# The transposed state of a chunked recurrence: by a transposition stage, or by a second product with swapped operands, in a chain of four stages

## The chip, the cores and the metric

The kernel runs on one core of a Trainium2 chip. The metric is the device time of one execution in microseconds (us). It is measured over several executions, and the median is given. One further execution is recorded by the hardware profiler; all lines of the profile are from that one.

## What is computed

Two parts follow each other. The first is a recurrence over 768 tokens for 4 x 8 = 32 heads, each with a state of 40 x 40; the second is a dense layer pair of 320 x 2048 and 2048 x 320 over all 3072 tokens, with a piecewise quadratic activation between.

```python
def _attn_ref(r, k, v, w, a, b):              # each 4 x 8 x 768 x 40, f32
    state = np.zeros((B, H, D, D))
    for t in range(S):
        y[:, :, t] = np.einsum('bhd,bhde->bhe', rt, state)
        Sa = np.einsum('bhde,bhe->bhd', state, at)
        state_decay = state * wt[:, :, None, :] - np.einsum('bhd,bhe->bhde', Sa, bt)
        state = state_decay + np.einsum('bhd,bhe->bhde', vt, kt)
...
def _moe_ref(x, w_in, w_out):                 # 3072 x 320, 320 x 2048, 2048 x 320
    h = x @ w_in
    g = np.where(h >= 1, h, np.where(h <= -1, 0.0, (h + 1) ** 2 / 4))
    return g @ w_out
```

## The kernel before

**Chunks and halves.** The 768 tokens are cut into 24 chunks of 32. The heads are handled in two halves of 16. For one half of one chunk, `chain(c, hb)` (line 441) makes the output of the chunk and the state for the next chunk. It is a Python generator: each `next` on it issues one stage, up to the next `yield`. All matrix work in it is on small f32 tiles, one or two matmuls for each of 16 heads; the profile counts every f32 matmul as two instructions, so a group of 16 shows as x32.

The five stages of the chain before are:

1. L456: 16 products into one PSUM tile, and L460, a ScalarE copy into `x0`.
2. L466: 16 products with the inverted 32 x 32 matrices `tinv`. VectorE (L473) and ScalarE (L477) then take turns to put the results into the operand tile `cg`, four instructions each, from one PSUM tile.
3. L484: 16 products with all 128 rows, which give both the chunk's output (columns 0 to 31) and the new state (columns 32 to 71). VectorE scales the state by the decay into the next chunk's operand tile `cn` (L491, four instructions) and the output into `yt` (L496, two).
4. L513: the new state, 40 x 40 for each head, is transposed by a product with an identity; ScalarE copies it to `ss` (L517). `round_y` (L502) splits the output into two parts for the dense layers, on ScalarE and GpSimd.
5. L523: 16 products of the transposed state with the next chunk's rows `pn`; ScalarE copies the result to `cn` (L525, two instructions). With that, stage 1 of the next chunk can start.

**What feeds the chain.** For each half chunk, `load_cg` and `load_ti` issue DMAs on SyncE's queue that bring rows from a scratch buffer in DRAM, `turn` (parts 0, 1, 2) makes three groups of 32 x 32 transposes on VectorE (L410, L413, L415), and `scores` makes 32 small products (L425) and masks them on VectorE (L434). There are three operand tiles `cg`, so that a half chunk is loaded while two others are in use.

**The dense layers** are the generator `moe()` (line 558). A group is 64 tokens of each batch row, 256 columns; there are 12 groups. For each of 16 blocks of 128 hidden units, TensorE makes eight matmuls of 256 columns into `ph` (L594; two such PSUM tiles take turns), ScalarE applies Relu and Square (L600, L601), and six matmuls of 320 columns (L568, L572) of the block two before are made. Then VectorE finishes the activation (L607), which is also the last reader of `ph`, so the block after next cannot begin its L594 before that L607. ScalarE (L581) and GpSimd (L582) split the activation into two parts. `feed(cols)` (line 809) draws matmuls from this generator until their columns, counted by its `yield`s, reach what is owed. In one chunk's time 30720 columns are owed, which is half a group, so the dense layers keep pace with the chain. They start in chunk 2 with a delay, and end after it.

**Background.** `background(n)` draws from three more generators for later chunks: `rows` (running products of the decays on VectorE, L234 and L243, products on GpSimd, loads and a store), `ab` (32 x 32 transposes L278, products L289) and `inv` (triangular inversion on GpSimd, L314 and L320). Each has windows of time in tenths of a chunk (`WINDOWS`), and `SHARE` says how a chunk's share is spread over its ten steps. `adopt` (L328) turns an inverse into `tinv` every fourth chunk. `pull(wgen, 2)` draws from the conversion of the dense weights, which is done in the first chunks.

**What sets the order.** The order of each engine's instructions is that in which the code issues them (`manual_schedule`); each engine works its queue in order. The loop at line 833 has ten steps in a chunk. A step is one stage of one half, and then three times 1024 columns of the dense layers and a slice of the background. Odd steps belong to half 0, even ones to half 1; in steps 2 and 4 that is still half 1 of the chunk before.

All short-lived PSUM tiles come from one pool of four (`psum()`, line 62).

## Time and profile before

| What | us |
|---|---|
| median of 3 runs | 941.84 (938.14 to 942.95) |
| the profiled execution | 939.9 |
| its span, first to last instruction | 937.4 |
| TensorE busy in the span | 740.5 |
| VectorE busy in the span | 606.9 |
| ScalarE busy, GpSimd busy | 456.3, 428.4 |

The span is 2.5 us less than the time of the profiled execution, since it leaves out what lies ahead of the first and behind the last instruction. PE stands for TensorE, PEld for its weight loads, DVE for VectorE, ACT for ScalarE, POOL for GpSimd, SP for SyncE. A row of the timeline gives the start, how long it took, the engine, line and operation, `out<-in`, the sizes, how many equal instructions are merged, and in brackets how long the engine had stood idle and what ended that. Matmuls overlap, so the durations of rows that follow each other run a little into one another. The "PEclk" column is the granted TensorE clock as a share of full speed.

### The profile page before, as it was taken

The page shows a single profiled execution, that of the slowest core. Times are in us where ns is not written, and L with a number is a line of the kernel's source. Part 1 is how long each engine was busy: PE and PEld are TensorE (multiplying, and loading weights), DVE is VectorE, ACT ScalarE, POOL GpSimd, SP SyncE. Part 2 cuts the span into 40 slices and gives each one's busy share as a digit, 9 for nine tenths or more (in the row PEclk, how much of TensorE's full clock was granted, in tenths as well). Part 3 has the DMA queues.
Part 4 walks back from the last instruction along what each step waited for, and adds up shares of the span by engine and source line. Part 5 has one row for each costly group of instructions (what it writes and reads, how often), then busy time and mean ns, then how long its engine had stood idle before and what let it go on. Part 6 is the DMA issues. An engine that isn't in the chain of part 4 may idle for free.

```text
span 937.4 us, 35480 instructions
## 1 busy us (share of the span) xinstructions
PE 740.5 (79%) x14976; PEld 654.3 (70%) x14976; DVE 606.9 (65%) x1574; ACT 456.3 (49%) x1182; POOL 428.4 (46%) x673
## 2 busy tenths in 40 slices
PE   4343542348988986988796988899999999999995
PEld 3232532337877875877785977788888888888895
DVE  5787877577766784777755776666766566665321
ACT  5453444123444433545353544446556555656663
POOL 4300223677323696334695332796226952223332
PEclk9565555577977989899899889989999999999998
DMA  9299993665896556786467685575733554451000
GB/s 305 55 199 254 218 221 103 143 135 122 185 190 142 136 132 120 150 183 141 77 146 140 125 183 115 102 164 103 144 89 71 120 102 95 84 110 37 19 30 14
DMA packets 223167, 122.01 MB, mean 130 GB/s; under 512 B 142825, under 2 KB 214697, under 8 KB 223009
## 3 DMA queue, kind: packets, MB, share of 16 engines
q1 hardware_dynamic: 219808, 108.61, 54.5%
q0 software_dynamic: 3200, 11.14, 3.9%
q8 instruction: 117, 1.92, 0.9%
q14 instruction: 42, 0.34, 0.1%
HBM read 90.54 MB, written 27.53 MB: 126 GB/s over the span
## 4 chain that ended last, share of the span: by engine, by line
PE 37%; DVE 23%; DMA 12%; POOL 8%; ACT 7%; issue 6%; SPq 6%; DVEq 0%; ACTq 0%; POOLq 0%
PE ph L594 12%; PE po L568 7%; PE p L484 4%; PE po L572 4%; DVE arena L234 3%; PE p L513 3%; DVE cg L473 3%; SPq L265 3%; DVE qt L607 2%; DVE rec L243 2%; ACT cg L477 2%; POOL lw L314 2%; POOL lw L320 2%; DMA ti<-scr 2%; DMA ld_a<-in_a_dram 2%
## 5 line engine op out<-in xcount | busy, mean ns | idle before, releaser
L594 PE MATMUL ph<-X,w 120*128 120x256 f32 x1536 | 260.2, 305 | 62.3 <-DVE qt L607 61.1
L582 POOL TENSOR_TENSOR gl<-qt,gh 128x256 fp32r<-128x256 f32 x192 | 141.2, 736 | 299.4 <-ACT gh L581 284.5
L594 PEld LDWEIGHTS ph<-X,w 120*128 120x128 f32 x1536 | 215.4, 200 | 83.0 <-DVE qt L607 67.9
L568 PE MATMUL po<-wide,gh 128*128 128x320 f32 x768 | 161.9, 327 | 0.3 <-ACT gh L581 0.3
L607 DVE SCALAR_TENSOR_TENSOR qt<-qt,ph 128x256 f32<-128x256 f32 x192 | 79.9, 416 | 124.0 <-ACT qt L601 111.9
L581 ACT CAST gh<-qt 128x256 fp32r<-128x256 f32 x192 | 78.0, 406 | 160.3 <-DVE qt L607 159.7
L477 ACT ACTIVATE cg<-p 32x160 f32<-32x160 f32 x192 | 56.5, 294 | 149.5 <-DVE cg L473 149.5
L568 PEld LDWEIGHTS po<-wide,gh 128*128 128x128 f32 x768 | 123.2, 200 | 3.6 <-ACT gh L581 0.5
L484 PE MATMUL p<-cg 128*64 128x72 f32 (+1 forms) x1536 | 74.4, 259 | 44.2 <-ACT cg L477 43.5
L473 DVE SCALAR_TENSOR_TENSOR cg<-p,mask 32x128 f32<-32x128 f32 x192 | 55.3, 288 | 78.5 <-ACT cg L477 52.0
L572 PE MATMUL po<-wide,gl 128*128 128x320 f32 x384 | 97.9, 333 | 7.9 <-POOL gl L582 7.7
L484 PEld LDWEIGHTS p<-cg 128*64 128x64 f32 x1536 | 65.6, 163 | 55.0 <-ACT cg L477 46.0
L600 ACT ACTIVATE qt<-ph,half_c 128x256 f32<-128x256 f32 x192 | 90.9, 473 | 20.2 <-POOL gl L582 14.3
L434 DVE TENSOR_TENSOR cg<-p,mask 32x256 f32<-32x256 f32 x192 | 80.6, 420 | 19.2 <-PE p L425 16.4
L320 POOL TENSOR_TENSOR lw<-lw 128x31 f32<-128x31 f32 (+15 forms) x155 | 83.7, 540 | 8.3
L601 ACT ACTIVATE qt<-qt 128x256 f32<-128x256 f32 x192 | 80.2, 418 | 6.1
L314 POOL TENSOR_TENSOR lw<-lw 128x31 f32<-128x31 f32 (+15 forms) x155 | 78.8, 509 | 8.5
L491 DVE SCALAR_TENSOR_TENSOR cg<-p,pr 40x160 f32<-40x160 f32 x184 | 59.1, 321 | 28.4 <-PE p L484 26.4
L572 PEld LDWEIGHTS po<-wide,gl 128*128 128x128 f32 x384 | 65.2, 195 | 13.4 <-POOL gl L582 10.6
L513 PE MATMUL p<-ident,cg 40*64 40x40 f32 x1472 | 57.5, 238 | 1.5 <-issue 1.5
L513 PEld LDWEIGHTS p<-ident,cg 40*64 40x64 f32 x1472 | 51.8, 146 | 3.6 <-issue 1.6
L466 PE MATMUL p<-x,tinv 32*32 32x72 f32 x1536 | 38.5, 242 | 10.8 <-DVE tinv L328 8.7
(106 smaller groups left out, 997.4 us busy)
## 6 DMA issues: line engine op xcount, KB each, us to landing
ti<-scr SPq DMA_DIRECT2D x96, 200.0 KB
ti<-scr SPq DMA_DIRECT2D x96, 168.0 KB
scr<-arena POOLq DMA_DIRECT2D x16, 640.0 KB, 5.6
cg<-scr SPq DMA_DIRECT2D x96, 80.0 KB
X<-Y SPq DMA_DIRECT2D x36, 160.0 KB
scr<-wide SPq DMA_DIRECT2D x8, 640.0 KB
tiab<-scr SPq DMA_DIRECT2D x32, 160.0 KB
scr<-in_r_dram SPq DMA_DIRECT2D x24, 160.0 KB
```

What stands on the lines that cost most here:

```text
L314: eng.tensor_mul(t3, W3[:, 0:n, j : j + 1].broadcast_to([128, n, m]), L3[:, j + 1 :, j].unsqueeze(1).broadcast_to([128, n, m]),)
L320: eng.tensor_sub(W3[:, 0:n, j + 1 :], W3[:, 0:n, j + 1 :], t3)
L434: nc.vector.tensor_tensor(out=cg[q, f::2, C_X : C_X + 64][:, 4 * i : 4 * i + 4].rearrange("p h (j x) -> p h j x", x=32), in0=ps[quarter(f, ...
L473: nc.vector.scalar_tensor_tensor(out=cg[q, f + 2 * i :: 4, C_R : C_R + 32], in0=psv[quarter(f, i), :, 0:32], scalar=-1.0, in1=mask[quarter ...
L484: nc.tensor.matmul(psv[h // 8][64 * f : 64 * f + 64, h // 2 % 4, 0:n3], lhsT=cgw[:, h * CW + C_G : h * CW + C_G + 64], rhs=cg[:, h, C_R : ...
L513: nc.tensor.matmul(pst[64 * f : 64 * f + 64, p, :], lhsT=cn[er[f], h, C_S : C_S + 64], rhs=ident[er[f]], start=True, stop=True)
L568: nc.tensor.matmul(pos[i], lhsT=gh[:, ts_], rhs=w2[f // 8][:, j, f % 8, :], start=f == 0 and j == 0, stop=False)
L572: nc.tensor.matmul(pos[i], lhsT=gl[:, ts_], rhs=w2[f // 8][:, 0, f % 8, :], start=False, stop=f == NF - 1)
L582: nc.gpsimd.tensor_sub(gl, gt, gh.bitcast(F32))
L594: nc.tensor.matmul(ph, lhsT=w1[:, wi, fs], rhs=Xs[g][:, xi, :], start=i == 0, stop=i == 7)
L600: nc.scalar.activation(gt, ph, AF.Relu, bias=half_c, scale=0.5)
L607: nc.vector.scalar_tensor_tensor(out=gt, in0=gt, scalar=1.0, in1=ph, op0=ALU.min, op1=ALU.max)
```

## The change

The transposition stage goes. The state is made by a product of two operands, and the same product with its operands swapped gives its transpose, so stage 3 now makes both: 16 new products (L486 of the changed kernel) into one PSUM tile, copied by ScalarE to `ss` in two instructions of 40 partitions (L491), ahead of the products that give output and state (now L497). The decay, which the transposed copy lacks, is applied where the last stage's result is taken out of PSUM: VectorE does that now (L528, two instructions of 40 x 256), in place of ScalarE's copy (L525 before). `round_y` moves to that stage. Stage 2 writes two PSUM tiles, so that VectorE and ScalarE read different ones at a time.

The loop over chunks now has four parts instead of ten steps. In each, two stages are issued one behind the other, one of each half, which stand two stages apart: third and first, fourth and second. Behind them stand the loads, `turn`, `scores` and `adopt`, and then `fill()`: six times 1280 columns of the dense layers, each with a slice of the background. `SHARE` has four entries. The columns in a chunk stay 30720, and `pull(wgen, 2)` is drawn 12 times in a chunk, not 10.

```diff
-SHARE = (3.1, 1.45, 0.93, 2.03, 0.6) * 2
+SHARE = (1.4, 0.6) * 2
+SLOTS = len(SHARE)
...
-        psv = psum()[:, 0:288].rearrange("p (h x) -> p h x", x=72)
+        psv = [psum()[:, 0:288].rearrange("p (h x) -> p h x", x=72) for _ in range(2)]
...
-                psv[quarter(f, p % 2), p // 2, :], lhsT=tinv[q : q + 32, c % 4, 4 * hb + p // 2, :],
+                psv[p % 2][quarter(f, p % 2), p // 2, :], lhsT=tinv[q : q + 32, c % 4, 4 * hb + p // 2, :],
...
         yield
+        if not last:
+            pst = psum()[:, 0:320].rearrange("p (h x) -> p h x", x=40)
+            for h in range(16):
+                nc.tensor.matmul(
+                    pst[er[h % 2], h // 2, :], lhsT=cg[:, h, C_S : C_S + D], rhs=cg[:, h, C_G : C_G + D], start=True, stop=True
+                )
+            ss = work.tile([128, 8, 40], F32, tag="ss", name="ss", bufs=1)
+            for rows in er:
+                nc.scalar.copy(ss[rows], pst[rows])
         psv = psum_2()
...
-        pst = psum()[:, 0:320].rearrange("p (h x) -> p h x", x=40)
-        for h in range(16):
-            f, p = h % 2, h // 2
-            nc.tensor.matmul(
-                pst[64 * f : 64 * f + 64, p, :], lhsT=cn[er[f], h, C_S : C_S + 64], rhs=ident[er[f]], start=True, stop=True
-            )
-        ss = work.tile([128, 8, 40], F32, tag="ss", name="ss", bufs=1)
-        nc.scalar.copy(ss, pst)
-        round_y()
-        yield
...
         for f in range(2):
-            nc.scalar.copy(cn[er[f], f::2, C_R : C_R + 32], psv[er[f]])
+            nc.vector.scalar_tensor_tensor(
+                out=cn[er[f], f::2, C_R : C_R + 32], in0=psv[er[f]], scalar=-1.0,
+                in1=pr[er[f], :, 1, 39:40].broadcast_to([D, 8, 32]), op0=ALU.mult, op1=ALU.mult,
+            )
+        round_y()
         yield
...
+    def fill():
+
+        for k in range(6):
+            feed(1280)
+            if k % 2 == 0:
+                pull(wgen, 2)
+                if first:
+                    first.pop(0)()
+            background(now[0] + 10 / SLOTS * (k + 1) / 6)
+        now[0] += 10 / SLOTS
```

The loop over chunks after the change, whole:

```python
    for c in range(NC + 1):
        nxt = c + 1 < NC
        if c < NC:
            gens[c, 0] = chain(c, 0)
            gens[c, 1] = chain(c, 1)
        stage(c - 1, 1)
        stage(c, 0)
        if 0 < c < NC:
            if c % 4 == 0:
                adopt(c // 4)
            for j in (1, 2):
                turn(c, 1, j)
            if nxt:
                load_ti(c + 1, 1)
        fill()
        stage(c - 1, 1)
        stage(c, 0)
        if 0 < c < NC:
            scores(c, 1)
        for g, (t0, nt) in enumerate(groups):
            if t0 + nt == 32 * c:
                reclaim(5 + g % 2)
                Xs[g] = relayout(g)
                if idle[0]:
                    owed[0], idle[0] = -TRAIL * 3072, False
        if c == NC:
            break
        if nxt:
            load_cg(c + 1, 0)
            turn(c + 1, 0, 0)
        fill()
        stage(c, 0)
        stage(c, 1)
        if nxt:
            for j in (1, 2):
                turn(c + 1, 0, j)
            if c + 2 < NC:
                load_ti(c + 2, 0)
        fill()
        stage(c, 0)
        stage(c, 1)
        if nxt:
            scores(c + 1, 0)
            load_cg(c + 1, 1)
            turn(c + 1, 1, 0)
        fill()
```

The rows below show the order in which instructions stand in an engine's queue, late in the program (about chunk 20), where no background is left on VectorE. First VectorE before, for about half a chunk: `cg_83` to `cg_85` are the three operand tiles, `ph_63` and `ph_64` the two PSUM tiles of the dense layers, `p_` tiles those of the pool of four.

```order
L434 TENSOR_TENSOR cg_85<-p_12120,mask 32x4x64 x4
L410 STREAM_TRANSPOSE cg_83<-ti_80 64x8x32 x2
L473 SCALAR_TENSOR_TENSOR cg_84<-p_12202,mask 32x4x32 x4
L607 SCALAR_TENSOR_TENSOR qt<-qt,ph_63 128x256
L413 STREAM_TRANSPOSE ev<-ti_80 128x512
L607 SCALAR_TENSOR_TENSOR qt<-qt,ph_64 128x256
L491 SCALAR_TENSOR_TENSOR cg_83<-p_12288,pr_87 40x4x40 x2
L491 SCALAR_TENSOR_TENSOR cg_83<-p_12289,pr_87 40x4x40 x2
L496 TENSOR_TENSOR yt<-p_12288,pr_87 128x128
L496 TENSOR_TENSOR yt<-p_12289,pr_87 128x128
L607 SCALAR_TENSOR_TENSOR qt<-qt,ph_63 128x256
L415 STREAM_TRANSPOSE pr_86<-ti_80 128x16x32
```

VectorE at the same place after the change (L614 is L607 of before, L477 is L473, L438 is L434, L414 to L419 are L410 to L415, L504 is L491, L528 is new):

```order
L417 STREAM_TRANSPOSE ev<-ti_80 128x512
L419 STREAM_TRANSPOSE pr_88<-ti_80 128x16x32
L614 SCALAR_TENSOR_TENSOR qt<-qt,ph_63 128x256
L614 SCALAR_TENSOR_TENSOR qt<-qt,ph_64 128x256
L528 SCALAR_TENSOR_TENSOR cg_85<-p_12990,pr_86 40x8x32 x2
L477 SCALAR_TENSOR_TENSOR cg_84<-p_13011,mask 32x4x32 x2
L477 SCALAR_TENSOR_TENSOR cg_84<-p_13012,mask 32x4x32 x2
L438 TENSOR_TENSOR cg_85<-p_13037,mask 32x4x64 x4
L414 STREAM_TRANSPOSE cg_83<-ti_81 64x8x32 x2
L614 SCALAR_TENSOR_TENSOR qt<-qt,ph_63 128x256
L614 SCALAR_TENSOR_TENSOR qt<-qt,ph_64 128x256
L504 SCALAR_TENSOR_TENSOR cg_83<-p_13144,pr_87 40x4x40 x2
```

Before, three or fewer groups of chain work stood between two activations of the dense layers; now the activations stand in pairs, and all of a part's chain work stands between two pairs. The first of a pair, on `ph_63`, belongs to the block that TensorE made last in the part before.

TensorE before, from one activation tile to the next (L425 is `scores`, L513 the transposition, L466 stage 2):

```order
L594 MATMUL ph_63<-X_1761,w_89 128x256 x4
L425 MATMUL p_12120<-cg_85,ev 32x32 x16
L425 MATMUL p_12120<-pr_88,ev 32x32 x16
L513 MATMUL p_12157<-ident,cg_85 64x40 x16
L594 MATMUL ph_63<-X_1761,w_89 128x256 x4
L568 MATMUL po_65<-wide_884,gh 128x320 x2
L568 MATMUL po_66<-wide_884,gh 128x320 x2
L572 MATMUL po_65<-wide_884,gl 128x320
L572 MATMUL po_66<-wide_884,gl 128x320
L466 MATMUL p_12202<-x_12083,tinv 32x72 x16
L594 MATMUL ph_64<-X_1761,w_89 128x256 x8
```

TensorE after, in a part with a third and a first stage (L486 are the swapped products, L497 output and state, L460 stage 1; L601, L575 and L579 are L594, L568 and L572):

```order
L486 MATMUL p_12112<-cg_83 40x40 x16
L497 MATMUL p_12132<-cg_83 64x72 x8
L497 MATMUL p_12133<-cg_83 64x72 x8
L460 MATMUL p_12157<-cg_84 32x72 x16
L601 MATMUL ph_64<-X_1823,w_89 128x256 x8
L575 MATMUL po_65<-wide_884,gh 128x320 x2
L575 MATMUL po_66<-wide_884,gh 128x320 x2
L579 MATMUL po_65<-wide_884,gl 128x320
L579 MATMUL po_66<-wide_884,gl 128x320
L601 MATMUL ph_63<-X_1823,w_89 128x256 x8
```

Chain and dense layers were interleaved in pieces of 3072 columns; now a part has its two stages first, and then two whole blocks of the dense layers (7680 columns), the one on `ph_64` and then the one on `ph_63`.

More of the change, by code (lines that the diff above doesn't have):

```diff
@@ L356, in window, with gone @@
         return WINDOWS[key][s - 1]
-    gone = lambda x: sum(SHARE) * (int(x) // 10) + sum(SHARE[: int(x) % 10]) + SHARE[int(x) % 10] * (x % 1)
+    def gone(x):
+        x = x * SLOTS / 10
+        i = int(x)
+        return sum(SHARE) * (i // SLOTS) + sum(SHARE[: i % SLOTS]) + SHARE[i % SLOTS] * (x - i)
     def background(n):
@@ L817, in feed, with stage @@
             idle[0] = d is None
-    def step(c, hb):
+    def stage(c, hb):
         if (c, hb) in gens:
             next(gens[c, hb], 0)
-        for k in range(3):
-            if (c, hb) in gens:
-                feed(1024)
-            if k == 0:
+    def fill():
+        for k in range(6):
+            feed(1280)
+            if k % 2 == 0:
                 pull(wgen, 2)
-            if first and k == 0:
-                first.pop(0)()
-            background(now[0] + (k + 1) / 3)
-        now[0] += 1
+                if first:
+                    first.pop(0)()
+            background(now[0] + 10 / SLOTS * (k + 1) / 6)
+        now[0] += 10 / SLOTS
     for c in range(NC + 1):
         nxt = c + 1 < NC
-        if 0 < c < NC and c % 4 == 0:
-            adopt(c // 4)
         if c < NC:
             gens[c, 0] = chain(c, 0)
-        if nxt:
-            load_cg(c + 1, 0)
-        step(c, 0)
+            gens[c, 1] = chain(c, 1)
+        stage(c - 1, 1)
+        stage(c, 0)
+        if 0 < c < NC:
+            if c % 4 == 0:
+                adopt(c // 4)
+            for j in (1, 2):
+                turn(c, 1, j)
+            if nxt:
+                load_ti(c + 1, 1)
+        fill()
+        stage(c - 1, 1)
+        stage(c, 0)
         if 0 < c < NC:
             scores(c, 1)
-        step(c - 1, 1)
         for g, (t0, nt) in enumerate(groups):
@@ L850, in rwkv_moe_kernel @@
                     owed[0], idle[0] = -TRAIL * 3072, False
[L851 to L856 removed]
         if c == NC:
             break
[L859 removed]
         if nxt:
[L861 removed]
+            load_cg(c + 1, 0)
+            turn(c + 1, 0, 0)
+        fill()
+        stage(c, 0)
+        stage(c, 1)
+        if nxt:
+            for j in (1, 2):
+                turn(c + 1, 0, j)
             if c + 2 < NC:
                 load_ti(c + 2, 0)
[L864 to L867 removed]
+        fill()
+        stage(c, 0)
+        stage(c, 1)
         if nxt:
             scores(c + 1, 0)
[L870 to L871 removed]
+            load_cg(c + 1, 1)
             turn(c + 1, 1, 0)
[L873 to L881 removed]
+        fill()
     for _ in mgen:
```

27 lines of the change are left out of this document (2 added, 25 removed).

## The prediction

> **What bounds the kernel now.** I read the page's busy times (in the table above), then the span cut into four stretches, then where the chunks stand, then the waits, and last the timeline of half a chunk. By its share of the span (79%) PE would be the bound throughout. The stretches (columns: stretch, length, busy time of PE, PEld, DVE, ACT, POOL, then granted clock, DMA share, GB/s) tell more:
>
> ```profile
> 71.00:246.00 175.00, 87.99 (x1840) 76.51 (x1833) 126.94 (x309) 65.37 (x158) 78.28 (x121) 0.63 0.76 173
> 246.00:640.00 394.00, 338.61 (x6957) 299.34 (x6948) 267.75 (x740) 180.64 (x488) 214.31 (x342) 0.90 0.66 140
> 640.00:861.00 221.00, 217.72 (x4720) 193.87 (x4709) 143.55 (x371) 130.36 (x349) 93.90 (x155) 1.00 0.48 98
> 861.00:938.00 77.00, 64.50 (x733) 61.09 (x732) 19.05 (x51) 42.50 (x107) 24.34 (x33) 0.96 0.07 23
> ```
>
> The edges are where the first stage (L456) of chunks 0, 4, 15 and 23 starts; the last three:
>
> ```profile
> 245.76 0.46 PE L456 MATMUL p<-cg 128*32 128x72 f32 x16
> 639.53 0.46 PE L456 MATMUL p<-cg 128*32 128x72 f32 x16
> 861.21 0.51 PE L456 MATMUL p<-cg 128*32 128x72 f32 x18
> ```
>
> So chunks 4 to 14 (the middle) take 393.8 us, 35.8 each, and chunks 15 to 22 (the late part) 221.7 us, 27.7 each. Late, PE never rests (217.7 of 221) and its clock is full. In the middle PE rests 55 of 394 us and its clock is 0.90. What it waits for (us, times, longest):
>
> ```profile
> PE ph L594 <- DVE qt L607: 61.1, 26, 10.9
> DVE cg L473 <- ACT cg L477: 52.0, 144, 0.4
> PE p L484 <- ACT cg L477: 43.5, 5, 19.3
> ```
>
> VectorE is late with the activation (L607) that frees a `ph` tile, because its queue holds other work ahead. An example from the middle:
>
> ```profile
> 452.54 0.41 DVE L607 SCALAR_TENSOR_TENSOR qt<-qt,ph 128x256 f32<-128x256 f32 x1
> 455.17 4.07 DVE L243 TENSOR_TENSOR rec<-rec,ld_w 128x40 f32<-128x40 f32 x7
> 462.36 0.42 DVE L607 SCALAR_TENSOR_TENSOR qt<-qt,ph 128x256 f32<-128x256 f32 x1
> 462.83 1.44 PE L594 MATMUL ph<-X,w 120*128 120x256 f32 x5 [5.10 <-DVE qt L607]
> ```
>
> Between two activations lie 9.8 us of VectorE, 4.07 of them background, and PE loses 5.10. **What decides is how much VectorE work stands in front of an activation, against how much PE work covers it.**
>
> Late, half a chunk looks like this, first VectorE and then the chain on PE:
>
> ```profile
> 714.52 1.72 DVE L434 TENSOR_TENSOR cg<-p,mask 32x256 f32<-32x256 f32 x4 [0.54 <-PE p L425]
> 716.27 0.91 DVE L410 STREAM_TRANSPOSE cg<-ti 64x256 f32<-64x256 f32 x2
> 717.78 0.29 DVE L473 SCALAR_TENSOR_TENSOR cg<-p,mask 32x128 f32<-32x128 f32 x1 [0.59 <-PE p L466]
> 720.04 0.42 DVE L607 SCALAR_TENSOR_TENSOR qt<-qt,ph 128x256 f32<-128x256 f32 x1
> 720.38 0.70 DVE L413 STREAM_TRANSPOSE ev<-ti 128x512 f32<-128x512 f32 x1
> 722.73 1.33 DVE L491 SCALAR_TENSOR_TENSOR cg<-p,pr 40x160 f32<-40x160 f32 x4 [0.47 <-PE p L484]
> 724.07 0.49 DVE L496 TENSOR_TENSOR yt<-p,pr 128x128 f32<-128x128 f32 x2
> 713.73 0.45 PE L425 MATMUL p<-cg,ev 40*32 40x32 f32 x32
> 714.41 1.13 PE L513 MATMUL p<-ident,cg 40*64 40x40 f32 x32
> 717.01 0.70 PE L466 MATMUL p<-x,tinv 32*32 32x72 f32 x32
> 719.38 0.80 PE L523 MATMUL p<-pr,ss 40*40 40x32 f32 x32
> 720.52 1.22 PE L594 MATMUL ph<-X,w 120*128 120x256 f32 x8
> 721.96 1.22 PE L484 MATMUL p<-cg 128*64 128x72 f32 x32
> 724.73 0.71 PE L456 MATMUL p<-cg 128*32 128x72 f32 x32
> ```
>
> The activation ends at 720.46 and L594 on that tile starts at 720.52: before is only just covered. A group's end overlaps the next by some 0.07 us, so the groups cost PE 0.68 (scores, two such rows up to 714.41), 1.06 (L513), 0.63 (L466), 0.73 (L523), 1.15 (L484) and 0.64 us (L456). One block of the dense layers costs 1.84, from row to row behind the chain:
>
> ```profile
> 886.69 1.12 PE L594 MATMUL ph<-X,w 120*128 120x256 f32 x8
> 888.53 1.12 PE L594 MATMUL ph<-X,w 120*128 120x256 f32 x8
> ```
>
> **The change, part by part.**
>
> *PE work.* 32 transposition instructions go, 32 swapped ones come. No row has them. Below stands L523 with 0.73 us (40 weight columns, 32 moving), above L484 with 1.15 (all 128 rows, 64 and 72). I take 0.73: with 40 and 40 columns it lies nearest to L523. That saves 0.33 us of PE in a half chunk, which counts only where PE sets the pace.
>
> [...]
>
> *Stage 2.* Each L473 now waits 0.36 us for ScalarE three times in four (144 waits, 52.0 us). With two PSUM tiles the engines run side by side: 4 x 0.29 and one wait of 0.15, 1.3 instead of 2.26 us.
>
> *Last stage.* L528 is new on VectorE. By its neighbours it takes between 0.32 (L491, 160 columns) and 0.43 us (L434, 256); with 256 columns I take 0.42, twice: 0.84.
>
> *The new wait.* In a part PE has its two stages, then a block on `ph_64`, then one on `ph_63`. That second block needs the activation of the `ph_63` before, and this now stands in VectorE's queue behind all the chain work of the part.
>
> Part with stages 4 and 2: L528 can start at 0.73 + 0.15 (the lag seen from L466 to L473) = 0.88. Then 0.84 + 1.3 + 1.72 (L434) + 0.91 (L410) + 0.42 (activation) = 5.19, so the block can start at 6.13. PE is there at 0.73 + 0.63 + 0.68 + 1.84 = 3.88 and waits 2.25. The part takes 6.13 + 1.84 = 7.97.
>
> Part with stages 3 and 1: L491 starts at 0.73 + 0.58 + 0.2 = 1.51; 1.33 + 0.49 + 1.40 (L413, L415) + 0.42 bring 5.15, the block starts at 5.2. PE is there at 0.73 + 1.15 + 0.64 + 1.84 = 4.36 and waits 0.85. The part takes 7.04.
>
> Together 15.0 a half chunk, **30.0 us a chunk**, against 27.7 late. Queued behind the activation are ScalarE's split (L581), its next Relu, and GpSimd's L582; PE reads what they make only after the eight matmuls of that block, so I add nothing for them.
>
> *The clock.* Waits of about 2 us can halve it:
>
> ```profile
> 316.66 1.90 PE L594 MATMUL ph<-X,w 120*128 120x256 f32 x8 [1.80 <-DVE qt L607]
> 410.85 1.23 PE L594 MATMUL ph<-X,w 120*128 120x256 f32 x8 [1.82 <-DVE qt L607]
> 210.97 1.15 PE L594 MATMUL ph<-X,w 120*128 120x256 f32 x4 [2.44 <-DVE qt L607]
> 608.57 0.74 PE L594 MATMUL ph<-X,w 120*128 120x256 f32 x4 [2.45 <-DVE qt L607]
> 310.00:320.00 10.00, 8.20 (x114) 7.07 (x114) 6.29 (x17) 5.81 (x17) 6.84 (x14) 0.84 0.55 106
> ```
>
> Of two waits of 1.8 us one is followed by matmuls at near twice their time, and of two of 2.4 us one. Where it happens, a 10 us stretch shows 0.84: 1.6 to 1.7 us lost. All that follows the wait is on the path, so I take half, 0.85 a half chunk, 1.7 a chunk: 31.7.
>
> *Background.* `SHARE` now puts 35% of a chunk's background into each part with stages 3 and 1.
>
> ```profile
> L243 DVE TENSOR_TENSOR rec<-rec,ld_w 128x40 f32<-128x40 f32 x112 | 39.1, 349 | 3.3
> L234 DVE TENSOR_TENSOR arena<-arena,ld_w 128x40 f32<-128x40 f32 x112 | 36.1, 323 | 3.1
> L278 DVE STREAM_TRANSPOSE ea<-tiab 128x256 f32<-128x256 f32 x64 | 23.8, 415 | 6.4 <-DMA tiab<-scr 6.3
> L328 DVE STREAM_TRANSPOSE tinv<-lw 128x1024 f32<-128x1024 f32 x6 | 12.1, 2018 | 0.0
> ```
>
> The first three make 99 us over about 13.5 chunks, 7.3 a chunk and 2.6 a part. VectorE has 7.04 + 0.88 - 5.15 - 0.42 = 2.35 us free there, so on average little is exposed; since it is uneven I take 0.5 a half chunk, between 0 and 2.6. The middle's transposes of 2 us (L328 and its like L303, three each) and its DMA waits add some 1.5 a chunk. Middle: 31.7 + 1.0 + 1.5 = 34.2.
>
> *Loads and SyncE, weights, GpSimd.* `load_cg` is issued three parts (some 22 us) ahead of its use instead of ten steps (27); late, DMA is half idle, so I put this at nothing. GpSimd's background is spread more evenly: nothing. More weight conversion a chunk, with fewer stages, in chunks 0 to 3: nothing, with 19 us either way, the longest of the five waits of L484 above.
>
> *Tail.* Chunk 23 has one more half with bursts: 2 us. Then the last relayout:
>
> ```profile
> 895.51 0.39 PE L594 MATMUL ph<-X,w 120*128 120x256 f32 x1 [0.38 <-DMA X<-Y]
> ```
>
> PE waited 0.38 for it, with 21504 columns of dense work issued behind the rounding; after, 15360 are left there, 1.6 blocks or 2.9 us less: 3 more.
>
> **Sum**, against the profiled execution of 939.9 us: late 8 x 31.7 + 4 (two `adopt`) - 221.7 = +36; middle 11 x 34.2 - 393.8 = -18; tail +5; early 0. That gives 963; the median of the runs is 1.9 above this execution, so **965 us**.
>
> **Rivals.**
>
> 1. *The waits cost no clock.* Then 1.7 goes from 19 chunks, 32 us: 933. For it: two of the four waits above. [...]
> 2. *Every wait costs it.* 32 us more: 997.
> 3. *The burst is hidden*, and PE sets the pace, so that the shorter products show: 0.66 a chunk late gives -5, half of the 55 us that PE rests in the middle -28, and the tail is as before: 909. Against it: late, before is covered by 0.06 us only, with 6 us of PE work for a burst of 5.9; after has 3.2 for 5.2.
> 4. *The swap saves nothing* (1.15 us instead of 0.73, which lies in the path of a part): 0.42 x 38 = +16: 981. It is part of my own range.
>
> Between 1 and 2 the share of waits that lose clock decides: none, half, all. Slower than before begins at about one in seven.
>
> **How the numbers follow.** My forecast, 945 to 982, has 0.57; rival 2 (982 to 1010) 0.16; rival 1 (922 to 945) 0.15; rival 3 (890 to 922) 0.12. A measurement of this kernel can tell about 0.5%, 4.7 us. Faster by more (under 937.1): rival 3 and two thirds of rival 1, 0.22. Within: 0.08. Slower: 0.70. The range 922 to 1000 leaves out rival 3 and the top of rival 2.
>
> **What would show it.** Right: late chunks of 30 to 33 us; "PE ph <- DVE qt L614" among the longest waits, nearly 2 us each in every other part; clock under 1.00 late; L486 near 0.73; no alternating waits in L477. Wrong: late chunks under 27 with PE at 100%; VectorE's activations early; the middle at 31 or less; a shift in chunks 0 to 3 of over 19 us.

## The result, and the profile after

The changed kernel takes **1040.63 us** (median of 4 runs, 1032.73 to 1043.19) against 942.06 for the one before: 1.104 times as long, 95% interval 1.097 to 1.111. The forecast was 965 us with a range to 1000, so the sign was right and the size was not. The profiled execution took 1041.47 us with a span of 1039.3.

The stretches of the changed kernel, cut where its first stage (L460) of chunks 0, 4, 15 and 23 starts, with the columns of the windows before:

```profile
71.00:266.80 195.80, 83.74 (x1870) 74.25 (x1863) 128.31 (x318) 63.38 (x152) 77.64 (x121) 0.59 0.71 157
266.80:687.80 421.00, 335.57 (x6934) 300.69 (x6930) 288.86 (x788) 173.90 (x469) 218.28 (x351) 0.86 0.61 130
687.80:960.40 272.60, 227.82 (x4742) 204.56 (x4742) 156.77 (x403) 123.44 (x332) 90.89 (x145) 0.91 0.40 80
960.40:1039.00 78.60, 64.34 (x706) 60.99 (x704) 20.25 (x53) 40.54 (x102) 23.66 (x32) 0.96 0.06 21
```

Every stretch is longer: the early part by 21 us (forecast 0), the middle by 27 (forecast -18), the late part by 51 (forecast +36), the tail by 3 (forecast +5). Late, PE was busy for 217.7 of 221 us before, at a clock of 1.00; now it rests 45 of 273 us, and its clock is 0.91.

Some waits of the changed kernel (us, times, longest): PE's for the activation and for GpSimd's part of the split, and two of other engines:

```profile
PE ph L601 <- DVE qt L614: 119.1, 71, 9.8
PE po L579 <- POOL gl L589: 24.3, 11, 11.8
DVE arena L231 <- DMA scr<-arena: 21.3, 3, 11.4
POOL arena L249 <- DMA ld_b<-in_b_dram: 13.1, 5, 7.7
```

PE's wait for the activation, L614 now, has grown from 26 times to 71 (61.1 us before) and is the longest that PE has; the other three have to do with the background, to which the last runs come back. ScalarE's alternation with VectorE in stage 2 is gone, as the prediction had it: VectorE waits 4.2 us for ScalarE there, where it was 52.0. Late, a part with stages 4 and 2 looks like this, PE first and then VectorE:

```profile
930.84 0.80 PE L526 MATMUL p<-pr,ss 40*40 40x32 f32 x32
932.89 1.21 PE L601 MATMUL ph<-X,w 120*128 120x256 f32 x8
936.97 1.64 PE L601 MATMUL ph<-X,w 120*128 120x256 f32 x8 [1.99 <-DVE qt L614]
938.40 1.27 PE L575 MATMUL po<-wide,gh 128*128 128x320 f32 x4
940.13 1.13 PE L486 MATMUL p<-cg 128*40 128x40 f32 x32
945.24 1.21 PE L601 MATMUL ph<-X,w 120*128 120x256 f32 x8 [0.28 <-DVE qt L614]
931.69 0.86 DVE L528 SCALAR_TENSOR_TENSOR cg<-p,pr 40x256 f32<-40x256 f32 x2 [1.15 <-PE p L526]
932.58 1.21 DVE L477 SCALAR_TENSOR_TENSOR cg<-p,mask 32x128 f32<-32x128 f32 x4
933.80 1.72 DVE L438 TENSOR_TENSOR cg<-p,mask 32x256 f32<-32x256 f32 x4
935.55 0.91 DVE L414 STREAM_TRANSPOSE cg<-ti 64x256 f32<-64x256 f32 x2
936.49 0.42 DVE L614 SCALAR_TENSOR_TENSOR qt<-qt,ph 128x256 f32<-128x256 f32 x1
```

The queue of VectorE is the one of the prediction, instruction by instruction: L528, L477, L438, L414, and only then the activation. From the start of stage 4 (930.84) to the block that waits (936.97) it is 6.13 us, the forecast to the hundredth. Behind this wait of 1.99 us, block and second products take 3.16 us to L486 at 940.13, where the prediction has 1.84 at full clock: the granted clock was 1.00 from 930.00 to 934.98, ahead of the wait, and 0.50 from 938.40 to 940.13. The part with stages 3 and 1 waits 0.28 us (the row at 945.24), less than the 0.85 summed. So the rows of a late part read as forecast. What they don't say is where the 76 us come from that the forecast lacks.

### The profile page after: what moved, and what is told of

It reads as the page before. It is cut to its first block, busy times and chain, and to the rows that moved or that the text cites. A ratio compares the mean times of both kernels' runs of the same rounds, so it can differ in the third digit from the quotient of the medians.

```text
span 1039.3 us, 35607 instructions
## 1 busy us (share of the span) xinstructions
PE 742.4 (71%) x14976; PEld 663.1 (64%) x14976; DVE 643.8 (62%) x1666; ACT 438.7 (42%) x1136; POOL 428.1 (41%) x673
## 4 chain that ended last, share of the span: by engine, by line
DVE 32%; PE 29%; DMA 12%; issue 10%; POOL 7%; SPq 6%; ACT 4%; DVEq 0%; ACTq 0%; POOLq 0%
PE ph L601 10%; PE po L575 5%; DVE cg L438 4%; DVE qt L614 3%; PE p L486 3%; PE p L497 3%; DVE cg L414 3%; DVE cg L504 3%; PE po L579 3%; DMA ti<-scr 2%; DVE arena L235 2%; DMA cg<-scr 2%; DVE cg L477 2%; POOL lw L321 2%; POOL lw L315 2%
## 5 line engine op out<-in xcount | busy, mean ns | idle before, releaser
L601 PE MATMUL ph<-X,w 120*128 120x256 f32 x1536 | 264.2, 321 | 125.6 <-DVE qt L614 119.1
L601 PEld LDWEIGHTS ph<-X,w 120*128 120x128 f32 x1536 | 225.0, 216 | 155.1 <-DVE qt L614 139.4
L589 POOL TENSOR_TENSOR gl<-qt,gh 128x256 fp32r<-128x256 f32 x192 | 141.2, 736 | 398.4 <-ACT gh L588 376.6
L575 PE MATMUL po<-wide,gh 128*128 128x320 f32 x768 | 160.8, 334 | 0.3 <-ACT gh L588 0.3
L614 DVE SCALAR_TENSOR_TENSOR qt<-qt,ph 128x256 f32<-128x256 f32 x192 | 79.2, 412 | 130.6 <-ACT qt L608 121.7
L575 PEld LDWEIGHTS po<-wide,gh 128*128 128x128 f32 x768 | 128.4, 208 | 2.0 <-ACT gh L588 0.5
L504 DVE SCALAR_TENSOR_TENSOR cg<-p,pr 40x160 f32<-40x160 f32 x184 | 59.2, 322 | 96.8 <-PE p L497 94.7
L579 PE MATMUL po<-wide,gl 128*128 128x320 f32 x384 | 96.5, 335 | 24.3 <-POOL gl L589 24.3
L607 ACT ACTIVATE qt<-ph,half_c 128x256 f32<-128x256 f32 x192 | 90.2, 470 | 19.6 <-POOL gl L589 14.0
L438 DVE TENSOR_TENSOR cg<-p,mask 32x256 f32<-32x256 f32 x192 | 80.6, 420 | 13.5 <-PE p L429 10.9
L579 PEld LDWEIGHTS po<-wide,gl 128*128 128x128 f32 x384 | 70.1, 207 | 28.8 <-POOL gl L589 28.7
L486 PE MATMUL p<-cg 128*40 128x40 f32 x1472 | 50.4, 240 | 46.7 <-ACT cg L481 40.7
L486 PEld LDWEIGHTS p<-cg 128*40 128x40 f32 x1472 | 43.9, 152 | 58.7 <-ACT cg L481 47.5
L497 PE MATMUL p<-cg 128*64 128x72 f32 (+1 forms) x1536 | 70.2, 255 | 0.0
L528 DVE SCALAR_TENSOR_TENSOR cg<-p,pr 40x256 f32<-40x256 f32 x92 | 38.7, 420 | 44.5 <-PE p L526 43.8
L497 PEld LDWEIGHTS p<-cg 128*64 128x64 f32 x1536 | 64.9, 163 | 0.4 <-issue 0.4
L477 DVE SCALAR_TENSOR_TENSOR cg<-p,mask 32x128 f32<-32x128 f32 x192 | 55.3, 288 | 10.4 <-ACT cg L481 4.2
```

The lines of the kernel that those rows point to most:

```text
L438: nc.vector.tensor_tensor(out=cg[q, f::2, C_X : C_X + 64][:, 4 * i : 4 * i + 4].rearrange("p h (j x) -> p h j x", x=32), in0=ps[quarter(f, ...
L486: nc.tensor.matmul(pst[er[h % 2], h // 2, :], lhsT=cg[:, h, C_S : C_S + D], rhs=cg[:, h, C_G : C_G + D], start=True, stop=True)
L497: nc.tensor.matmul(psv[h // 8][64 * f : 64 * f + 64, h // 2 % 4, 0:n3], lhsT=cgw[:, h * CW + C_G : h * CW + C_G + 64], rhs=cg[:, h, C_R : ...
L504: nc.vector.scalar_tensor_tensor(out=cn[er[f], f::2, C_S : C_S + D][:, halves[i]], in0=psv[i][er[f], :, 32:72], scalar=-1.0, in1=pr[er[f], ...
L575: nc.tensor.matmul(pos[i], lhsT=gh[:, ts_], rhs=w2[f // 8][:, j, f % 8, :], start=f == 0 and j == 0, stop=False)
L579: nc.tensor.matmul(pos[i], lhsT=gl[:, ts_], rhs=w2[f // 8][:, 0, f % 8, :], start=False, stop=f == NF - 1)
```

## The experiments

Line numbers move by a few from kernel to kernel, so rows are told apart by their operands. The table has all runs, by the span of the profiled execution and its stretches, cut by the first row of stage 1 of chunks 0, 4, 15 and 23; in brackets us a chunk.

| run | median, us | span | early | middle | late | tail |
|---|---|---|---|---|---|---|
| before | 942.06 | 937.4 | 174.7 | 393.8 (35.8) | 221.7 (27.7) | 76.2 |
| after | 1040.63 | 1039.3 | 195.4 | 421.0 (38.3) | 272.5 (34.1) | 78.9 |
| e1_act_early | 949.61 | 948.5 | 187.4 | 385.9 (35.1) | 225.8 (28.2) | 78.4 |
| e2_chain_in_old_loop | 928.00 | 925.5 | 177.1 | 383.6 (34.9) | 220.0 (27.5) | 73.8 |
| e3_spin | 1028.68 | 1027.4 | 197.3 | 413.7 (37.6) | 264.5 (33.1) | 81.9 |
| e4_before_act_early | 949.75 | 947.9 | 174.2 | 396.6 (36.1) | 229.2 (28.6) | 76.4 |
| e5_early_cg | 958.64 | 950.0 | 188.2 | 385.8 (35.1) | 228.4 (28.6) | 76.9 |
| e6_share_even | 947.48 | 945.3 | 186.9 | 388.5 (35.3) | 220.0 (27.5) | 78.4 |
| e7_share_b | 959.07 | 959.2 | 185.6 | 393.0 (35.7) | 230.6 (28.8) | 78.4 |
| e8_fewer_pulls | 952.03 | 947.8 | 182.6 | 387.3 (35.2) | 227.8 (28.5) | 79.8 |
| f1_after_no_background | 896.27 | 895.4 | 140.9 | 351.9 (32.0) | 251.1 (31.4) | 78.9 |
| f2_act_early_no_background | 767.43 | 766.1 | 133.5 | 281.2 (25.6) | 201.6 (25.2) | 79.7 |
| f3_before_no_background | 801.43 | 799.6 | 137.7 | 298.1 (27.1) | 216.6 (27.1) | 76.4 |
| f4_after_no_inverse | 1010.84 | 1007.1 | 188.3 | 402.5 (36.6) | 266.8 (33.4) | 78.9 |
| g1_after_no_rows | 962.25 | 963.9 | 158.8 | 381.9 (34.7) | 273.2 (34.1) | 79.8 |
| g2_after_rows_only | 962.12 | 960.0 | 173.2 | 382.3 (34.8) | 253.6 (31.7) | 78.6 |
| g3_no_background_spin | 870.20 | 869.6 | 143.0 | 332.5 (30.2) | 240.6 (30.1) | 83.4 |

### Is it the activation's place in the queue?

**e1_act_early.** In the changed kernel, the activation moves ahead of the second products:

```diff
                 yield 15 * n // 16
+                nc.vector.scalar_tensor_tensor(out=gt, in0=gt, scalar=1.0, in1=ph, op0=ALU.min, op1=ALU.max)
                 while len(late) > (2 if g and f == 2 else 1):
                     yield from second(*late.pop(0))
...
-                nc.vector.scalar_tensor_tensor(out=gt, in0=gt, scalar=1.0, in1=ph, op0=ALU.min, op1=ALU.max)
```

> The changed kernel; the activation L614 of a block is issued right behind the block's Square, ahead of the six second products, so that the activation of the part's last block stands on VectorE ahead of the next part's chain work. Theory Q (the place of L614 in VectorE's queue, and the clock lost in that wait, set the pace of a part): the waits 'PE ph <- DVE qt L614' go, late chunks fall from 34.1 to 27 to 28.5 us with a clock near 1.00, the middle from 38.3 to 33 to 36, the early part stays: 935 us, 915 to 965. Rival P (the products and VectorE's work of the four stages themselves set the pace: swapped products on all rows, L528 on VectorE): late chunks stay over 31 us, 1000 us or more. Rival C (queue order yes, but PE then waits for the chain itself at the stages): late chunks 29 to 31, 960 to 990.

Measured: 949.61 us, ratio 1.012 (1.007 to 1.017). One moved line takes back 91 of the 102 us of span. Late and middle fall as the theory of the queue had it; the early part, which was to stay, falls by 8 us as well. The late timeline of this kernel, PE and then VectorE (the activation is L610 here):

```profile
826.59 1.21 PE L601 MATMUL ph<-X,w 120*128 120x256 f32 x8
828.51 1.12 PE L601 MATMUL ph<-X,w 120*128 120x256 f32 x8
830.45 0.81 PE L486 MATMUL p<-cg 128*40 128x40 f32 x32
831.08 1.20 PE L497 MATMUL p<-cg 128*64 128x72 f32 x32
832.21 0.71 PE L460 MATMUL p<-cg 128*32 128x72 f32 x32
824.85 0.42 DVE L610 SCALAR_TENSOR_TENSOR qt<-qt,ph 128x256 f32<-128x256 f32 x1 [1.77 <-ACT qt L608]
825.38 0.86 DVE L528 SCALAR_TENSOR_TENSOR cg<-p,pr 40x256 f32<-40x256 f32 x2
```

The activation now stands ahead of L528, and the second block follows the first after 1.92 us with no wait. The group L486 takes 0.63 us to the next, so the swapped products cost a little less than the 0.73 forecast. In both timelines VectorE took up its work in the order of the code: L528 at 931.69, then L477, L438, L414 and the activation at 936.49 in the changed kernel, and here the activation at 824.85, then L528 at 825.38.

**e2_chain_in_old_loop.** The kernel before, with `chain()` as in the change's diff and all else (loop, `SHARE`, `feed`) as it was.

> The kernel before with the new chain alone (swapped products, two PSUM tiles in stage 2, L528's like on VectorE, rounding in the last stage); loop, SHARE and feed as before, the fifth step of a half chunk issues no stage. Theory Q: the chain edit is no part of the loss, since each step still has one stage of a half chunk: 0.7 us a late chunk less PE work, no alternating waits in stage 2, 930 us, 918 to 942. Rival P (the chain's own work is what costs): 960 us or more. If the early part's +21 us belongs to the loop, chunks 0 to 3 take 175 us as before; if to the chain, about 195.

Measured: 928.00 us, ratio 0.988 (0.984 to 0.992). It is 1.2% faster than the kernel before. The chain edit is worth 12 us of span, 10 of them in the middle; the early part is 2 us longer. So the loss, and 18 of the early part's 21 us, belong to the loop, or to the loop and the chain together: the new loop with the old chain was not run. Late it gives only 0.2 us a chunk of the some 0.9 that the swapped products save (1.06 less 0.63, twice). PE waits for the activation (L610 here) 39 times in it, 26 before:

```profile
PE ph L597 <- DVE qt L610: 70.8, 39, 11.4
```

**e4_before_act_early.** The same moved line in the kernel before.

> The kernel before with the activation L607 issued right behind its Square, as in the first run of this set. Theory Q: late, before is covered already, so late chunks stay at 27.7; of the 61 us of waits for L607 in the middle those go that stand behind the chain, not those behind background: 925 us, 910 to 938. Rival (in before the place of the activation is of no account): 938 to 944.

Measured: 949.75 us, ratio 1.011 (1.007 to 1.016), 1.1% slower, so neither theory held. PE's wait for the activation does go down by half, from 61.1 us to 32.1, but VectorE, which has to wait for ScalarE's Square at that place, now waits longer, ahead of the chain work that stands behind it in the queue (the activation is L603 here):

```profile
DVE qt L603 <- ACT qt L601: 177.1, 126, 4.4
```

Before, the same wait is 111.9 us, 92 times. VectorE stands still 65 us more, PE 29 us fewer for it, and the sum is a loss of 10.5 us of span. So the early place is not good in itself; it is good where a burst stands behind it.

### Is it the clock?

**e3_spin.** In the changed kernel, fifteen products on PE that nobody reads, in the wait of each part with stages 4 and 2:

```diff
                 fs = slice(128 * f, 128 * f + 128)
+                spin = psum()[:, 0:n] if part[0] and f % 2 == 0 else None
+                for _ in range(part[0] * (f % 2 == 0)):
+                    nc.tensor.matmul(spin, lhsT=w1[:, 0, fs], rhs=Xs[g][:, 0, :], start=True, stop=True)
```

> The changed kernel, and in each part with stages 4 and 2 fifteen idle products (1.6 us at full clock) on PE between the block on ph_64 and that on ph_63, into a PSUM tile that nobody reads: they fill the wait of 2 us and remove none of it. They stand on PE alone, so that the activation still comes when it comes. Theory Q with the clock: the block behind the wait runs at full clock, a part with stages 4 and 2 falls from 9.3 to 8.0 to 8.3 us late, late chunks from 34.1 to 31.5 to 32, the whole to 990 us, 975 to 1005. Rival (the lost clock is not due to the wait, or costs nothing on the path): 1035 us or more, late chunks 34 or more.

Measured: 1028.68 us. The fifteen products, for which the expectation has 1.6 us, an estimate of the author's that no run shows, took 2.15 us a time (94.6 us for 660 of them). The clock rises from 0.91 to 0.97 late, but a late chunk falls by 1.0 us and one of the middle by 0.7, not by 2. Neither theory had that. A likely reason is the background, which is mixed into these chunks; g3 below is the same run without it.

### Loads, shares and conversions

Four runs on top of e1 asked what else of the loop could be at fault. **e5_early_cg** issues both `load_cg` one part earlier; **e6_share_even** and **e7_share_b** add other values of `SHARE` to that; **e8_fewer_pulls** is e5 with 20 weight conversions a chunk in place of 24. The lines that differ, taken together from these runs (the second `load_cg` moves in the same way, and e7 has `SHARE = (0.6, 1.4) * 2`):

```diff
-SHARE = (1.4, 0.6) * 2
+SHARE = (1, 1) * 2
...
             if nxt:
                 load_ti(c + 1, 1)
+        if nxt:
+            load_cg(c + 1, 0)
         fill()
...
         if nxt:
-            load_cg(c + 1, 0)
             turn(c + 1, 0, 0)
...
-                pull(wgen, 2)
+                pull(wgen, 2 if k else 1)
```

> The first run of the study (changed kernel, activation early; early part 187.4 us, middle 35.1 and late 28.2 us a chunk) with both load_cg one part earlier, so four parts ahead of their use. Theory L: in chunks 0 to 3 the DMA engines are full and load_cg comes too late (PE waits 6.8 us for a DMA ahead of the first L486 of chunk 1); the early part falls to 177 to 181, the rest stays: 940 us, 935 to 945. Rival: the loads are hidden as the prediction had it, and the early part's loss is the weight conversion's: 947 to 952.

> The run before this one in the same set, with SHARE = (1, 1) * 2: half of a chunk's background in each kind of part instead of 70% with stages 3 and 1. Theory S (the background comes in lumps that VectorE's slack in a part doesn't cover, the term that the prediction took too low): the middle falls by 1 to 2 us a chunk, the late part with background (chunks 15 to 19) too: 15 to 30 us less than that run. Rival (background costs by its waits across engines, PE and GpSimd behind L279 and L589, wherever it stands): within 5 us of that run. Rival (parts with stages 4 and 2 are full already): 5 to 20 us more.

> As the run before this one, but SHARE = (0.6, 1.4) * 2: 70% of the background in the parts with stages 4 and 2. Theory S with a part's slack: parts with scores have 1.7 us more VectorE work, so this is 10 to 25 us slower than SHARE (1, 1). Rival (place is of no account): within 5 us of it.

> The first run of this set (load_cg early) with five weight conversions a part instead of six, 20 a chunk as in the kernel before. Theory W (24 conversions a chunk stand ahead of the chain's work on ScalarE in chunks 0 to 3): the early part falls by 3 to 8 us, the total by as much. Rival (the prediction's: the stalls there take them in): within 3 us.

Measured: e5 958.64 us, no better than e1 in the early part (188.2 against 187.4); the theory of late loads falls. Its median lies above the rival's 952 too, which stays unexplained; the profiled execution, 952.29, is its fastest. e6 takes 947.48, 11 us less than e5 by the medians and 4.7 by the spans: the late part gains 8, the middle loses 3. That is between its theories, which had 15 to 30 less or no more than 5. e7 takes 959.07, as the theory of the lumps had it against e6. So the spread over the parts moves some 10 us, mostly late. e8 takes 952.03, 6.6 less than e5 by the medians and 2.2 by the spans. Its early part is 5.6 us shorter than that of e5, and 3.0 shorter than that of e7, the shortest of those with 24 conversions: the four further conversions a chunk cost some 3 to 6 us there. None of these is the missing 76 us: in all of them, and in the kernel before, a chunk of the middle takes 35 to 36 us.

### The parts alone, and the background alone

If every loop takes 35 us a chunk in the middle, what stands there may not be the loop. Three kernels leave out the background, with its loads and stores (rows and products of the groups behind the second, inverses and `adopt` behind the first; the chunks read the first group's rows). f1 is the changed kernel, f2 is that with the activation early (e1), f3 is the kernel before. The edit of f1 and f3, and beside the moved line that of f2:

```diff
     def background(n):
+        return
...
     def drain(key, s):
+        if s > 0:
+            return
...
     def adopt(s):
+        if s > 0:
+            return
...
-        sc = scr4[c // 4][c % 4][hsel]
+        sc = scr4[0][c % 4][hsel]
```

> The changed kernel without the background work (rows, products and inverses of the token groups behind the first, and adopt's transposes behind it, are left out; the chunks read the first group's rows, so loads for the chunks stay). What is left in a chunk is the two kinds of part as the prediction's first sum has them: 30.0 us a chunk without lost clock, 31.7 with. Theory B (the prediction mis-sized the background, +2.5 us a chunk in the middle and +0.5 late, where the runs show some 8 and 4): middle and late both 30 to 31.5 us a chunk, middle 330 to 347 us in place of 421. Rival (the parts themselves are longer in the middle, by weights, loads or clock): middle 35 us a chunk or more. Theory B with the third kernel of this set: the difference to it in the middle is 3 to 4.5 us a chunk.

> As the first kernel of this set, with the activation issued early. Theory B: PE sets the pace, 24.3 us a chunk as in the chunks 19 and 21 of the first run of the study, in the middle too: 267 to 280 us for it. Rival (something in the middle other than background stops PE): 30 us a chunk or more.

> The kernel before without the same background work. Theory B: 27 to 28 us a chunk in the middle as in its late part, so 297 to 310 us in place of 394; 8 us a chunk is what background costs in the old loop. Rival: 32 us a chunk or more, because the waits for L607 in the middle stand behind the chain and not behind background.

Measured: 896.27, 767.43 and 801.43 us. The windows of the middle and the late part, for f1, f2 and f3 in turn:

```profile
213.50:565.40 351.90, 302.19 (x6166) 272.22 (x6162) 200.60 (x529) 169.57 (x455) 81.50 (x111) 0.93 0.40 83
565.40:816.50 251.10, 214.94 (x4484) 193.54 (x4480) 146.10 (x385) 121.91 (x328) 58.76 (x80) 0.95 0.39 80
```

```profile
203.70:484.80 281.10, 271.60 (x6164) 253.83 (x6162) 199.84 (x531) 170.31 (x454) 81.69 (x111) 0.99 0.50 103
484.80:686.40 201.60, 196.97 (x4484) 183.59 (x4480) 145.03 (x385) 123.07 (x329) 58.96 (x81) 1.00 0.48 100
```

```profile
208.50:506.60 298.10, 294.65 (x6162) 263.18 (x6162) 181.64 (x482) 179.04 (x476) 81.09 (x111) 1.00 0.47 97
506.60:723.10 216.50, 214.19 (x4481) 191.41 (x4480) 132.61 (x353) 129.45 (x345) 58.77 (x81) 1.00 0.45 93
```

Without background, middle and late are alike in each kernel: 27.1 us a chunk before, with PE at rest for some 1%; 32.0 and 31.4 after; 25.6 and 25.2 with the activation early. f3 came out as theory B had it; f1's middle (352 for 330 to 347) and f2's (281 for 267 to 280) lie just above their ranges, far from their rivals. The change costs 96 us of span without background and 102 with it. Turned round, the background costs 138 us of span before and 144 after: it is not the new loop that makes it dear. In the middle its price, with less without, is 95.7 us before, 69.1 after, and 104.7 in e1. The 69.1 are made up of three things. PE rests 35.7 us more (85.4 against 49.7). The background's own products on PE (L290, 768 instructions in this stretch) take 10.9. The other 22.5 are the rest of the matmuls taking longer, about what the clock makes of them by an estimate: 302.19 us at 0.93 would be 327 at 0.86, and 324.7 were measured.

> The changed kernel without background (896 us; 32.0 us a chunk in the middle, 31.4 late) and with fifteen idle products on PE in the wait of each part with stages 4 and 2, as in the third run of the study. Theory K (behind the wait of 2 us the clock is lost, 1.7 us a chunk by the prediction): 29.3 us a chunk in both, 6.8 and 7.9 to 8.15 us a part: 840 to 860 us. Rival (no clock lost, the parts just are that long): 890 or more.

**g3_no_background_spin** is f1 with e3's products. Measured: 870.20 us, 26 less than f1 and 10 more than the end of the range expected; its tail is 4.5 us longer. The parts, from the starts of stages 3 and 4 over 37 half chunks (chunks 4 to 22), take 6.66 and 8.42 us, against 6.99 and 8.87 in f1. The rows of g3, with L604 the products that nobody reads, and its middle and late windows:

```profile
763.55 0.75 PE L577 MATMUL po<-wide,gh 128*128 128x320 f32 x4
764.44 1.96 PE L604 MATMUL p<-X,w 120*128 120x256 f32 x15
766.57 1.22 PE L606 MATMUL ph<-X,w 120*128 120x256 f32 x8 [0.18 <-DVE qt L619]
767.63 0.75 PE L577 MATMUL po<-wide,gh 128*128 128x320 f32 x4
...
213.10:545.60 332.50, 319.27 (x6496) 292.96 (x6492) 200.87 (x530) 167.25 (x453) 81.25 (x111) 1.00 0.42 87
545.60:786.20 240.60, 231.97 (x4724) 212.93 (x4720) 145.75 (x385) 121.05 (x329) 58.65 (x81) 1.00 0.41 84
```

With the wait filled, the second products start 1.06 us behind the block, not 1.43 as from 936.97 to 938.40 above, and the clock is 1.00 in both stretches, for 0.93 and 0.95 in f1. So without background the wait does cost clock: 1.8 us a chunk in the middle, 1.3 late. With background, e3 got back 0.7 and 1.0. By part: of the 37 parts with stages 4 and 2, 19 are over 0.3 us longer in f1 than in g3, and 16 are equal within 0.02.

### Which background?

Three kernels leave out one part of it each: GpSimd's steps of the inverses behind the first (f4), the rows of the groups behind the second (g1), and all but the rows (g2).

```diff
-            eng.tensor_mul(
+            if s == 0:
+              eng.tensor_mul(
...
-            eng.tensor_sub(W3[:, 0:n, j + 1 :], W3[:, 0:n, j + 1 :], t3)
+            if s == 0:
+              eng.tensor_sub(W3[:, 0:n, j + 1 :], W3[:, 0:n, j + 1 :], t3)
```

```diff
     def prelude(s):

         reclaim(8)
+        yield 10
+        return
...
-        sc = scr4[c // 4][c % 4][hsel]
+        sc = scr4[min(c // 4, 1)][c % 4][hsel]
```

```diff
     def drain(key, s):
+        if s > 0 and key != "rows":
+            return
...
-        for key in ("inv", "ab", "rows"):
+        for key in ("rows",):
```

> The changed kernel without GpSimd's products and differences of the inverses behind the first (L315 and L321, 35 us of GpSimd for each of the groups; their transposes and all the rest stay). Theory G (the background's price comes from GpSimd, whose inverse stands ahead of L589, for which PE waits 24.3 us in all): middle 2 to 3 us a chunk less, late with chunks 17 and 18 down to 31: 1000 to 1015 us. Rival V (the price comes from VectorE's background and the waits for DMA): within 8 us of the changed kernel, 1030 to 1042.

> The changed kernel without the background's rows of the groups behind the second (L235, L244, L231 and the like on VectorE, three products on GpSimd, their loads and stores); products L290 and inverses stay and read the second group. All background together costs 144 us of span (1039 against 895 without), GpSimd's inverses 32 of it. Theory R (rows are the largest part, 75 us of VectorE in 2 and 3 us runs and the waits for DMA in VectorE's and GpSimd's queues): 60 to 90 us less, 950 to 980. Rival (products, their transposes and the inverses, which PE waits for itself): 20 to 45 us less, 995 to 1020.

> The changed kernel with the rows alone: products L279 and L290, inverses and adopt behind the first group are left out. If the parts add up, this and the run before it together save the 144 us once: by theory R 55 to 85 us less than the changed kernel, 955 to 985; by the rival 100 to 125 less, 915 to 940.

Measured: 1010.84, 962.25 and 962.12 us, all in the ranges of theories G and R, though f4's middle gains 1.7 us a chunk and not 2 to 3. GpSimd's part of the inverses costs 32 us of span, the rows 75, products and inverses together with `adopt` 79. The last two make 155, 11 more than all at once, so they nearly add up. g1 leaves out the loads and stores of the rows too, so how much of the 75 us is VectorE's, GpSimd's or the DMA engines' was not separated. g1's early part and g2's late part show where each stands:

```profile
70.20:229.00 158.80, 80.23 (x1846) 70.65 (x1846) 105.58 (x250) 64.34 (x153) 63.73 (x105) 0.65 0.70 149
627.90:881.40 253.50, 217.67 (x4482) 196.16 (x4480) 146.00 (x385) 122.20 (x328) 58.64 (x80) 0.93 0.38 80
```

The rows cost 37 us early, the products and inverses 19 us late. In the middle each costs 39 us. One example from the early part of the changed kernel shows a way in which it is paid beyond its busy time, by queues that stand behind a wait; PE, then GpSimd, then VectorE:

```profile
204.41 1.27 PE L575 MATMUL po<-wide,gh 128*128 128x320 f32 x4
217.46 0.90 PE L579 MATMUL po<-wide,gl 128*128 128x320 f32 x2 [11.79 <-POOL gl L589]
207.41 0.86 POOL L249 TENSOR_TENSOR arena<-ld_b,rec 128x320 f32<-128x320 f32 x1 [7.73 <-DMA ld_b<-in_b_dram]
...
209.53 0.69 POOL L321 TENSOR_TENSOR lw<-lw 128x255 f32<-128x255 f32 x1
...
216.06 0.67 POOL L321 TENSOR_TENSOR lw<-lw 128x247 f32<-128x247 f32 x1
216.69 0.72 POOL L589 TENSOR_TENSOR gl<-qt,gh 128x256 fp32r<-128x256 f32 x1
213.84 0.20 DVE L231 TENSOR_TENSOR arena<-ld_a,arena 128x40 f32<-128x40 f32 x1 [11.36 <-DMA scr<-arena]
214.18 4.10 DVE L235 TENSOR_TENSOR arena<-arena,ld_w 128x40 f32<-128x40 f32 x7
```

GpSimd's product L249 waits 7.73 us for a load, the store behind it sends off `arena` only then, and VectorE's next row L231 waits 11.36 us for that store. Meanwhile L589, which PE needs, stands on GpSimd behind L249 and nine steps of an inverse (209.53 to 216.06), and PE loses 11.79 us. It is a single place; the waits were not summed up by this cause.

## Why the prediction was wrong, point by point

| Term | forecast | measured | from |
|---|---|---|---|
| a chunk with its waits, at full clock | 30.0 us | 30.2 middle, 30.1 late | g3 |
| clock lost in the waits, a chunk | 1.7 us | 1.8 middle, 1.3 late | f1 less g3 |
| background, a chunk of the middle | 2.5 us | 6.3 us | after less f1 |
| background in the late part | 4 us (two `adopt`) | 21 us | after less f1 |
| early part | 0 | +21 us | after less before |
| tail | +5 us | +3 us | after less before |

- **The new wait: right.** The activation stands behind the part's chain work, PE waits some 2.0 us in each part with stages 4 and 2, and a chunk of the parts alone takes 30.1 us where 30.0 was summed. By kind the parts take 8.42 and 6.66 us, for 7.97 and 7.04 in the sum: two errors of 0.4 us that cancel, which is luck. e1 shows that the place in the queue is the cause: with that line moved, 91 us go, and 129 where there is no background (f1 against f2).
- **The clock: right without background, in size and in how often.** The prediction took half of the waits at 1.7 us each; 19 of 37 lost clock (over 0.3 us longer in f1 than in g3), and it came to 1.3 to 1.8 us a chunk. The half was a choice made from four rows, so that it fits this well is in part luck, and with background e3 got back only 0.7 to 1.0 us a chunk. Rivals 1 (no wait costs clock) and 2 (each does) are both refuted by f1 and g3. The row at 936.97 is one that lost it; taken for all, it would have put much of the miss on this term, where e3 and g3 show that it doesn't belong.
- **The background: wrong, and this is the step that failed.** The prediction built the middle anew, from the parts and what it took the background to expose there, 2.5 us a chunk. For that it held VectorE's background against VectorE's free time in a part (2.35 us against 2.6) and added some transposes and waits for DMA. GpSimd's background was put at "nothing", and the background's products on PE had no term. The runs without background show 6.3 us a chunk in the middle after, and 8.7 before. Of the 6.3, PE's own products are 1.0 (10.9 us over 11 chunks), and without GpSimd's steps of the inverses the middle falls by 1.7 a chunk (f4). The profile before had the price: its middle took 35.8 us a chunk and its late part 27.7. The prediction read this difference off the waits for L607, and since its sum starts from the new parts, the difference in effect went with the old loop. f3 shows that it belongs to the background: without it, the old loop's middle takes 27.1 as its late part does, and PE's waits for the activation in the whole program fall from 61.1 us to 8.1. A carried-over difference of 8.1 would have given 31.7 + 8.1 = 39.8 us a chunk in the middle, where 38.3 was measured, and +44 in place of -18: 1025 us.
- **Late: chunks 15 to 19 still have background.** The prediction gave them two `adopt`. Before, it costs 5 us in the late part (221.7 against 216.6), after 21: with the new loop, the late part is no longer the quiet one. 19 of it are products and inverses (g2).
- **Early: wrong.** "nothing, with 19 us either way" was argued from cover. 3.2 us come without background (140.9 against 137.7), 17.5 are background's (54.5 against 37.0). Another split of the same 21 us, with background in place: the activation's place makes some 8 (e1), the four further conversions a chunk 3 to 6 (e8, on top of e5), and `load_cg` none (e5).
- **The chain edit: right in sign.** In the old loop it gains 1.2% (e2), with swapped products at 0.63 us and stage 2 without alternation. Rival 4 (the swap saves nothing) falls.
- **Rival 3, a hidden burst, is what e1 does without background**, 25.2 to 25.6 us a chunk, with PE setting the pace. Against before that is 33 us of span (766 against 800); the background takes it back: it costs 182 us of span there (e1 less f2) and 138 before. Why it costs more there was not separated; that PE has no rest left behind which a stalled queue could hide is a guess.

The terms add up to the miss: middle 421.0 against 376 (+45), late 272.5 against 257.6 (+15), early +21, tail -2, together 79 from 963 us, where 1041.5 was measured.

## What to carry to other kernels

When a loop is rewritten around a background that stays, carry over what that background costs now, read from a stretch with it against one without (here 35.8 against 27.7 us a chunk), rather than the busy time that seems left over on one engine: of the 69.1 us that it cost here in the middle, 10.9 were its work on PE, and the rest were PE's added waits and lost clock. When stages are put together into bursts, see which release of a buffer comes to stand behind the burst, and issue it ahead of it. Test a chain edit and a loop edit apart: here the one gained 12 us and the other lost 114.

## What the runs showed of the hardware

- Waits of PE of some 2.0 us were followed by lost clock in 19 of 37 cases with the same work around them: these parts were over 0.3 us longer in f1 than in g3, where 1.96 us of products filled the wait, and the granted clock was 0.93 and 0.95 in f1 (middle and late), 1.00 in g3. In the changed kernel, behind the wait of 1.99 us that ends at 936.97, it was 0.50 from 938.40 to 940.13. What sets apart the waits that lose clock from those that don't was not shown.
- The 32 instructions of the swapped products, on all 128 rows with 40 weight and 40 moving columns, took 0.63 us in e1 (L486, from 830.45 to 831.08), 20 ns each; the group beside them with 64 and 72 columns took 1.13 us (L497, from 831.08 to 832.21), 35 ns each. In both groups the code sends consecutive products to two different halves of the PSUM partitions, and no run tried them on one half, so whether that counts for these times is open.
- The same matrix work, less the transposition stage, took less time in four bursts (f2) than in ten steps (f3). Without background a chunk takes 25.6 and 25.2 us in f2 (middle and late) and 27.1 in f3, with PE at rest for some 1 to 3% in both. Single late chunks with background show it too: 24.3 us in e1 (chunks 19 and 21, two of its shortest), and 27.1 and 26.7 before. The swap accounts for some 0.9 us of it; the rest was not taken apart, and that fewer changes between chain and dense blocks make it is a guess.
